# A third token block's output projection moved into the seven half-size products of the first two blocks, and those products moved later in the program

## The chip, the cores and the metric

The kernel runs on one core of one Trainium2 chip. Its time is in device microseconds. Engines are named as the profile names them: PE is TensorE (its matmuls), PEld its weight loads, DVE is VectorE, ACT ScalarE, POOL GpSimd, SP SyncE, which here only issues DMAs.

## What is computed

Two independent results are laid side by side. The first is attention with 32 query heads and one key and value head over 2048 tokens, followed by the output projection `@ wo`. The second is a two-dimensional Fourier transform by matrices, of which the real part is kept.

```python
q = (x @ wq).reshape(B, S, 32, 32).transpose(0, 2, 1, 3)
p = softmax(einsum("bhqd,bkd->bhqk", q, x @ wk) * 32 ** -0.5)
a = einsum("bhqk,bkd->bhqd", p, x @ wv).transpose(0, 2, 1, 3).reshape(B, S, 1024) @ wo
re, im = einsum("bsd,ed->bse", xb, hid_re), einsum("bsd,ed->bse", xb, hid_im)
b = einsum("ts,bse->bte", seq_re, re) - einsum("ts,bse->bte", seq_im, im)
return concatenate([a, b], axis=-1)
```

## The kernel before

Every large product is a sum of 128 x 128 by 128 x 512 matmuls in a reduced float format. To keep float32 accuracy, both operands are split into a high and a low part, and three matmuls are made of each pair: high by high, high by low, low by high. In the profile's names the right-hand parts are `rh` and `rl` (512 columns), the left-hand parts `mh` and `ml` (four 128 x 128 blocks in one tile), and the sum stands in a PSUM bank `psb`. I call one such matmul a fill. A group of fills fills one bank: eight row blocks by three give 24 fills, four row blocks by three give 12.

Attention runs in 32 units (4 token blocks `b` of 512 tokens, 8 groups `g` of 4 heads) of 32 steps. A step makes two score matmuls for the row maxima (`pss`, read by a reduction on DVE and an exponential on ACT), two score matmuls for the probabilities (`pst`, an exponential on ACT writes `p`), and, 3 times in a unit, a product of the probabilities with `v` (name `psb<-p,v`), which I call an attention product. DVE adds these into `ov`, and POOL multiplies by the inverse row sums `rb`. `level` (line 932) puts fills between the steps, so that a linear goal is met; the last 44 steps make no `pss` any more and take one fill more each.

The fills stand in one list `groups`, in this order: query projection, stage 1 and stage 2 of the Fourier part, and the output projection. Stage 1 and 2 use recursions that trade a product for additions. Stage 2 has seven products (`PRODUCTS`), each of 16 groups of 24 fills. The output projection of token blocks 0 and 1 uses the same kind of recursion (`OUTPUT`): the 8 token tiles are two halves of `MO` = 4 tiles, and seven half-size products of `MO` groups of 12 fills take the place of eight. Its left operands are sums of two tiles of the attention output, its right operands are sums of blocks of `wo`, split ahead by `w_parts`. `MID` is the place in stage 2's groups where these products are put in: behind 48 groups, so behind its third product. Token block 2 and then token block 3 use `o_group` instead: 8 groups of 24 fills for each block, with left operands that are stored already split (`oh`, `ol`), and right operands `wo_set`, 8 items of `wo` for each half of the columns.

Operands are made in two lines of work, `RL` for right-hand items and `ML` for left-hand ones. An item is loaded by a DMA of SP (`r`, `m`), two sources are added on POOL, POOL casts to the high part (`hi_r`, `hi_m`) and subtracts to get the low part (`lo`). The staging buffers `r` and `m` form rings of 3 (`NR0`, `NM0`, line 141), the split parts rings of `NR` = 14 right-hand and `NM` = 4 left-hand items (line 142). An item is due by its place among the fills (`due`), and `pump` takes the next steps when their time has come. Every engine's instructions are kept in the order in which the program writes them (line 79), SP's DMAs too, so an instruction that waits holds up all behind it on its engine.

Behind a finished group of stage 2's second half, DVE adds the bank to the first half's sum (`y<-y,psb`) and POOL adds or subtracts that into stored results (`y<-y,y`, twice for the last product). Behind all steps, the last 8 groups (block 3) run alone on PE: `first_part` takes 21 of the 24 fills, and the last 3 use the output of the last attention unit, which DVE splits.

Of the kernel before, what the change touches and what calls it, by code (L numbers as in the profile page):

```python
# [22 lines left out]
NG = 8  # L23
NQ = 4
NC = 16
MO = 4
MID = 3 * 16
ND = D // P


# [71 lines left out]
def tile_kernel(ctx: ExitStack, tc, xT, wq, wkv, wo, xbT, wT, cT, out):  # L102
# [12 lines left out]
    dram = ctx.enter_context(tc.tile_pool(name="dram", bufs=1, space=DRAM))  # L115
    qh_d = [[dram.tile([P, W], F32, name=f"qh_{b}_{g}") for g in range(NG)] for b in range(NQ)]
    ql_d = [[dram.tile([P, W], F32, name=f"ql_{b}_{g}") for g in range(NG)] for b in range(NQ)]
    o_d = [dram.tile([4, P, NG, P], F32, name=f"o_{b}") for b in range(2)]
    oh_d, ol_d = ({b: dram.tile([4, P, NG, P], F32, name=f"{n}_{b}") for b in (2, 3)} for n in ("oh", "ol"))
    w_d = [[[dram.tile([P, W], F32, name=f"w{q}_{n}_{c}") for q in range(2)] for c in range(4)] for n in range(len(OUTPUT))]  # L120
    c_d = {(i, e): [dram.tile([P, W], F32, name=f"c{i}{e}_{k}") for k in range(MO)] for i in range(2) for e in range(2)}
    r_d = [dram.tile([NC, P], F32, name=f"r_{u}") for u in range(NQ * NG)]
# [455 lines left out]
    def wo_set(e):  # L578
        return [Item([(lambda g=g: wo[g * P:(g + 1) * P, e * W:(e + 1) * W], 1)]) for g in range(NG)]
# [36 lines left out]

    got, made = [], []

    def o_products():

        seen = {}
        total = {(i, e): sum((i, e) == o[:2] for p in OUTPUT for o in p[2]) for i in range(2) for e in range(2)}
        for f, (lt, rt, outs) in enumerate(OUTPUT):
            def l_src(i, j, k):
                b, t = divmod(i * MO + k, 4)

                def src():
                    assert all(("o", b, g) in ready for g in range(4 * j, 4 * j + 4)), (b, t, j)
                    return o_d[b][t][:, 4 * j:4 * j + 4]
                return src  # L630

            R = [Item(None, pre=lambda f=f, c=c: have(("w", f, c), w_d[f][c])) for c in range(4)]
            for it in R:
                it.ahead = 24
            for k in range(MO):
                left = [Item([(l_src(i, j, k), sg) for i, j, sg in lt])]
                ys, plan = [], []
                for i, e, sg in outs:
                    n = seen.get((i, e, k), 0)
                    seen[i, e, k] = n + 1  # L640
                    it = None
                    if n:
                        it = Item([(lambda i=i, e=e, k=k, n=n: have(("c", i, e, k, n), c_d[i, e][k]), 1)])
                        ys.append(it)
                    r0 = (i * MO + k) * P
                    end_ = n + 1 == total[i, e]
                    plan.append((it, sg, out[r0:r0 + P, e * W:(e + 1) * W] if end_ else c_d[i, e][k], None if end_ else ("c", i, e, k, n + 1)))

                def post(ps, plan=plan):
                    first = None  # L650
                    for it, sg, to, key in plan:
                        if it is None:
                            if first is None:
                                first = op.tile([P, W], F32, name="qh")
                                dve.tensor_copy(first, ps)
                            store(to, first, key)
                            continue

                        def more(it=it, sg=sg, to=to, key=key):
                            (dve.tensor_add if sg > 0 else dve.tensor_sub)(it.y, it.y, ps)  # L660
                            store(to, it.y, key)
                        if it is plan[0][0]:
                            more()
                        else:
                            hold(more)
                yield Group(left, R, post, ys=ys, part=([R], 0))
# [3 lines left out]
    def o_group(b, t, e, ws):  # L670
        def post(ps):
            r0 = b * W + t * P
            to = out[r0:r0 + P, e * W:(e + 1) * W]
            if b < NQ - 1:
                oo = op.tile([P, W], F32, name="qh")
                dve.tensor_copy(oo, ps)
                store(to, oo)
                return

            n = len(halves)  # L680
            halves.append(n)
            oo = pp.tile([P, 2, W], F32, name="p")
            if n + 1 < 8:
                if n % 2:
                    dve.tensor_copy(oo[:, 0], ps)
                else:
                    act.activation(oo[:, 0], ps, AF.Copy)
                move(act, to, oo[:, 0])
                return
            for k, q in enumerate((act, sp)):  # L690
                cols = slice(k * W // 2, (k + 1) * W // 2)
                if k:
                    dve.tensor_copy(oo[:, k, :W // 2], ps[:, cols])
                else:
                    act.activation(oo[:, k, :W // 2], ps[:, cols], AF.Copy)
                move(q, to[:, cols], oo[:, k, :W // 2])
        return Group([o_left(b, t, q) for q in range(2)], ws, post)
# [10 lines left out]
    for it in st2[MID].right:  # L708
        it.back = 96
    rest += list(stage1()) + st2[:MID] + list(o_products()) + st2[MID:]  # L710
    w1, w0 = wo_set(1), wo_set(0)
    rest += [o_group(b, t, e, ws) for e, ws in ((1, w1), (0, w0)) for b in (2,) for t in range(4)]
    add(start + rest)
    w_parts(1010, 40)

# [103 lines left out]
    def pv(u, k):  # L819
# [11 lines left out]
        cur["at"] += 1  # L831
        if k == len(CUT) - 2:
            b, g = units[u]
            if b < 2:
                def scaled():
                    o = onp.tile([P, W], F32, name="oh")
                    gp.tensor_mul(o, ov[u], rb[u])
                    store(*blocks(o_d[b], g, o), ("o", b, g))
                ends.append(scaled)
                return  # L840
            hi_ = onp.tile([P, W], F32, name="oh").bitcast(F32R)
            lo_ = onp.tile([P, W], F32R, name="ol")
            lse["out"] = hi_, lo_

            last = u + 1 == len(units)
            e = dve if last else gp

            def low():
                e.tensor_sub(lo_, ov[u], hi_.bitcast(F32))
                if not last:  # L850
                    store(*blocks(oh_d[b], g, hi_))
                    store(*blocks(ol_d[b], g, lo_), ("o", b, g))

            ends.append(lambda: e.tensor_mul(ov[u], ov[u], rb[u]))
            ends.append(lambda: e.tensor_copy(hi_, ov[u]))
            ends.append(low)
# [82 lines left out]

    for n in range(total):  # L940
        u, r = divmod(n, SU)
        if n == total - 12:
            w1 = wo_set(1)
            add([o_group(NQ - 1, t, e, ws) for e, ws in ((0, w0), (1, w1)) for t in range(4)])
        score_step(n + SU + LEAD)
        if ends:
            ends.pop(0)()
        expo(n)
        if r == 16:
            inverse(u)  # L950
        if r in ENDS and n:
            pv((n - 1) // SU, (ENDS.index(r) - 1) % (len(CUT) - 1))
        level(n)
# [78 lines left out]
```

## Time and profile before

| | us |
|---|---|
| median of 3 runs | 2702.91 (2702.86 to 2704.59) |
| the profiled execution, its own time | 2701.05 |
| its span, first to last instruction | 2699.3 |
| PE busy in the span | 2691.8 |

The profiled execution is one execution. Its time is 1.75 us more than its span, and 1.86 us less than the median. A busy PE is read from matmul records whose ends are modelled, so the waits of PE and the spacing of matmuls are looked at beside it.

### The profile page before, as it was taken

The page shows a single profiled execution, that of the slowest core. Times are in us where ns is not written, and L with a number is a line of the kernel's source. Part 1 is how long each engine was busy: PE and PEld are TensorE (multiplying, and loading weights), DVE is VectorE, ACT ScalarE, POOL GpSimd, SP SyncE. Part 2 cuts the span into 40 slices and gives each one's busy share as a digit, 9 for nine tenths or more (in the row PEclk, how much of TensorE's full clock was granted, in tenths as well). Part 3 has the DMA queues.
Part 4 walks back from the last instruction along what each step waited for, and adds up shares of the span by engine and source line. Part 5 has one row for each costly group of instructions (what it writes and reads, how often), then busy time and mean ns, then how long its engine had stood idle before and what let it go on. Part 6 is the DMA issues. An engine that isn't in the chain of part 4 may idle for free.

```text
span 2699.3 us, 40577 instructions
## 1 busy us (share of the span) xinstructions
PE 2691.8 (100%) x13820; PEld 1918.1 (71%) x13820; DVE 1592.8 (59%) x1826; ACT 2134.8 (79%) x3131; POOL 1723.7 (64%) x1711
## 2 busy tenths in 40 slices
PE   9999999999999999999999999999999999999999
PEld 6876767676777767677776777667677776767767
DVE  5766666666666666565565656666565555655411
ACT  3588888888888888888888888888888888888741
POOL 4854425777547558765556675576887987865751
PEclk9999999999999999999999999999999999999999
DMA  8543336887788566564354588984675765644665
GB/s 277 190 136 128 114 97 202 282 285 233 241 268 281 203 226 195 175 193 142 125 160 152 183 258 278 306 262 128 213 226 161 223 199 159 209 142 134 192 211 187
DMA packets 316931, 538.24 MB, mean 199 GB/s; under 512 B 35962, under 2 KB 63354, under 8 KB 316666
## 3 DMA queue, kind: packets, MB, share of 16 engines
q1 hardware_dynamic: 315572, 533.69, 61.6%
q8 instruction: 109, 1.79, 0.3%
q10 hardware_dynamic: 1152, 1.97, 0.2%
q14 instruction: 98, 0.80, 0.1%
HBM read 395.58 MB, written 138.15 MB: 198 GB/s over the span
## 4 chain that ended last, share of the span: by engine, by line
PE 99%; ACT 0%; DVE 0%; DMA 0%; SPq 0%; issue 0%; ACTq 0%
PE psb L79 62%; PE pss L79 19%; PE pst L79 18%; ACT pss L79 0%; DVE nm L79 0%; DMA p<-in_xT_dram 0%; ACT p L79 0%; SPq L79 0%; DVE y L79 0%; DVE qh L79 0%; DVE rl L79 0%; ACT rh L79 0%; DVE p L79 0%; ACTq L79 0%
## 5 line engine op out<-in xcount | busy, mean ns | idle before, releaser
L79 DVE TENSOR_REDUCE nm<-pss 128x1 f32<-128x1024 f32 x1024 | 1252.5, 1223 | 562.0 <-PE pss L79 561.3
L79 ACT ACTIVATE p<-pst 128x1024 f32<-128x1024 f32 x1026 | 1056.6, 1030 | 437.7 <-PE pst L79 425.1
L79 ACT ACTIVATE pss<-pss,nm 128x1024 f32<-128x1024 f32 x1024 | 1114.7, 1089 | 57.2 <-DVE nm L79 55.5
L79 PE MATMUL psb<-rh,mh 128*128 128x512 f32 x1790 | 698.2, 390 | 0.3 <-ACT rh L79 0.3
L79 PE MATMUL psb<-rl,mh 128*128 128x512 f32 x1790 | 697.8, 390 | 0.6 <-DVE rl L79 0.5
L79 PE MATMUL psb<-rh,ml 128*128 128x512 f32 x1790 | 697.7, 390 | 0.0
L79 PE MATMUL pss<-kst,qst 128*128 128x512 f32 x2048 | 641.5, 394 | 0.2
L79 PE MATMUL pst<-qst,kst 128*128 128x512 f32 x2048 | 641.0, 394 | 0.5 <-ACT p L79 0.3
L79 POOL TENSOR_TENSOR ml<-m,mh 128x512 fp32r<-128x512 f32 x366 | 473.5, 1294 | 35.1 <-ACT mh L79 26.2
L79 PEld LDWEIGHTS pss<-kst,qst 128*128 128x128 f32 x2048 | 377.9, 188 | 125.4 <-issue 51.1
L79 PE MATMUL psb<-p,v 128*32 128x512 f32 x4096 | 459.3, 594 | 0.0
L79 PEld LDWEIGHTS pst<-qst,kst 128*128 128x128 f32 x2048 | 375.0, 188 | 103.0 <-ACT p L79 27.0
L79 PEld LDWEIGHTS psb<-rh,mh 128*128 128x128 f32 x1790 | 336.0, 188 | 75.6 <-ACT rh L79 1.8
L79 PEld LDWEIGHTS psb<-rl,mh 128*128 128x128 f32 x1790 | 336.0, 188 | 73.7 <-DVE rl L79 1.9
L79 PEld LDWEIGHTS psb<-rh,ml 128*128 128x128 f32 x1790 | 336.0, 188 | 71.1
L79 POOL CAST mh<-m 128x512 fp32r<-128x512 f32 x365 | 224.5, 615 | 229.1 <-PE psb L79 211.9
L79 PEld LDWEIGHTS psb<-p,v 128*32 128x32 f32 x4096 | 123.3, 110 | 283.0 <-issue 275.2
L79 POOL TENSOR_TENSOR m<-m,m 128x512 f32<-128x512 f32 x220 | 284.4, 1293 | 54.5 <-DMA m<-o 19.6
L79 POOL TENSOR_TENSOR rl<-r,rh 128x512 fp32r<-128x512 f32 x208 | 269.2, 1295 | 4.0
L79 POOL CAST rh<-r 128x512 fp32r<-128x512 f32 x208 | 129.0, 620 | 194.2 <-PE psb L79 147.3
L79 ACT ACTIVATION_READ_ACCUMULATOR pss<-pss,nm 128x1 f32 x1024 | 212.5, 207 | 0.0
L79 POOL TENSOR_TENSOR r<-r,r 128x512 f32<-128x512 f32 x120 | 155.1, 1293 | 52.3 <-DMA r<-in_wT_dram 33.6
(92 smaller groups left out, 791.3 us busy)
## 6 DMA issues: line engine op xcount, KB each, us to landing
m<-in_cT_dram SPq DMA_DIRECT2D x384, 256.0 KB
r<-s SPq DMA_DIRECT2D x192, 256.0 KB
y<-y SPq DMA_DIRECT2D x128, 256.0 KB
r<-in_wT_dram SPq DMA_DIRECT2D x88, 256.0 KB
m<-in_xbT_dram SPq DMA_DIRECT2D x88, 256.0 KB
y<-u SPq DMA_DIRECT2D x80, 256.0 KB
m<-in_wq_dram SPq DMA_DIRECT2D x64, 256.0 KB
qst<-qh SPq DMA_DIRECT2D x64, 256.0 KB
```

The source lines that it names most:

```text
L79: return lambda *a, **k: self.tc.keep_in_program_order(f(*a, **k))
```

## The change

Token block 2 joins the recursion. `MO` becomes 6: the 12 token tiles of blocks 0 to 2 are two halves of 6 (`token_tile` says which tile is which), and each of the seven products has 6 groups of 12 fills. Block 2's attention output is stored in float32 like that of blocks 0 and 1, so its split on POOL behind each unit goes, and its eight `o_group`s go. `MID` becomes 96: the seven products stand behind six products of stage 2, in front of the seventh. So stage 2's last product is the work that fills the last steps. Block 3 now makes both sets of `wo` items itself, and its groups are added 16 steps before the end of the steps, where it was 12.

```diff
--- before.py
+++ after.py
@@ -23,8 +23,8 @@
 NG = 8
 NQ = 4
 NC = 16
-MO = 4
-MID = 3 * 16
+MO = 6
+MID = 6 * 16
 ND = D // P
 
 
@@ -115,8 +115,8 @@
     dram = ctx.enter_context(tc.tile_pool(name="dram", bufs=1, space=DRAM))
     qh_d = [[dram.tile([P, W], F32, name=f"qh_{b}_{g}") for g in range(NG)] for b in range(NQ)]
     ql_d = [[dram.tile([P, W], F32, name=f"ql_{b}_{g}") for g in range(NG)] for b in range(NQ)]
-    o_d = [dram.tile([4, P, NG, P], F32, name=f"o_{b}") for b in range(2)]
-    oh_d, ol_d = ({b: dram.tile([4, P, NG, P], F32, name=f"{n}_{b}") for b in (2, 3)} for n in ("oh", "ol"))
+    o_d = [dram.tile([4, P, NG, P], F32, name=f"o_{b}") for b in range(3)]
+    oh_d, ol_d = ({b: dram.tile([4, P, NG, P], F32, name=f"{n}_{b}") for b in (3,)} for n in ("oh", "ol"))
     w_d = [[[dram.tile([P, W], F32, name=f"w{q}_{n}_{c}") for q in range(2)] for c in range(4)] for n in range(len(OUTPUT))]
     c_d = {(i, e): [dram.tile([P, W], F32, name=f"c{i}{e}_{k}") for k in range(MO)] for i in range(2) for e in range(2)}
     r_d = [dram.tile([NC, P], F32, name=f"r_{u}") for u in range(NQ * NG)]
@@ -616,13 +616,16 @@
 
     got, made = [], []
 
+    def token_tile(i, k):
+        return i * 4 + k if k < 4 else 4 + 2 * i + k
+
     def o_products():
 
         seen = {}
         total = {(i, e): sum((i, e) == o[:2] for p in OUTPUT for o in p[2]) for i in range(2) for e in range(2)}
         for f, (lt, rt, outs) in enumerate(OUTPUT):
             def l_src(i, j, k):
-                b, t = divmod(i * MO + k, 4)
+                b, t = divmod(token_tile(i, k), 4)
 
                 def src():
                     assert all(("o", b, g) in ready for g in range(4 * j, 4 * j + 4)), (b, t, j)
@@ -642,7 +645,7 @@
                     if n:
                         it = Item([(lambda i=i, e=e, k=k, n=n: have(("c", i, e, k, n), c_d[i, e][k]), 1)])
                         ys.append(it)
-                    r0 = (i * MO + k) * P
+                    r0 = token_tile(i, k) * P
                     end_ = n + 1 == total[i, e]
                     plan.append((it, sg, out[r0:r0 + P, e * W:(e + 1) * W] if end_ else c_d[i, e][k], None if end_ else ("c", i, e, k, n + 1)))
 
@@ -671,12 +674,6 @@
         def post(ps):
             r0 = b * W + t * P
             to = out[r0:r0 + P, e * W:(e + 1) * W]
-            if b < NQ - 1:
-                oo = op.tile([P, W], F32, name="qh")
-                dve.tensor_copy(oo, ps)
-                store(to, oo)
-                return
-
             n = len(halves)
             halves.append(n)
             oo = pp.tile([P, 2, W], F32, name="p")
@@ -708,8 +705,6 @@
     for it in st2[MID].right:
         it.back = 96
     rest += list(stage1()) + st2[:MID] + list(o_products()) + st2[MID:]
-    w1, w0 = wo_set(1), wo_set(0)
-    rest += [o_group(b, t, e, ws) for e, ws in ((1, w1), (0, w0)) for b in (2,) for t in range(4)]
     add(start + rest)
     w_parts(1010, 40)
 
@@ -831,7 +826,7 @@
         cur["at"] += 1
         if k == len(CUT) - 2:
             b, g = units[u]
-            if b < 2:
+            if b < NQ - 1:
                 def scaled():
                     o = onp.tile([P, W], F32, name="oh")
                     gp.tensor_mul(o, ov[u], rb[u])
@@ -939,8 +934,8 @@
 
     for n in range(total):
         u, r = divmod(n, SU)
-        if n == total - 12:
-            w1 = wo_set(1)
+        if n == total - 16:
+            w0, w1 = wo_set(0), wo_set(1)
             add([o_group(NQ - 1, t, e, ws) for e, ws in ((0, w0), (1, w1)) for t in range(4)])
         score_step(n + SU + LEAD)
         if ends:
```

Two stretches show how the instructions stand. The first is on POOL, in the last unit's steps, in the work that stands there beside the attention steps. Before, that is the end of stage 2's last product: one left-hand item's cast and subtraction, with the two additions into stored results between them.

```order
L79 CAST mh<-m_25431 128x512
L79 CAST rh<-r_25429 128x512
L79 TENSOR_TENSOR ml<-m_25431,mh 128x512
L79 TENSOR_TENSOR rl<-r_25429,rh 128x512
L79 CAST mh<-m_25470 128x512
L79 TENSOR_TENSOR y_25497<-y_25497,y_25495 128x512
L79 TENSOR_TENSOR y_25499<-y_25499,y_25495 128x512
L79 TENSOR_TENSOR ml<-m_25470,mh 128x512
```

Now, in the same product, the items of the `wo` set that was added at the 16th step from the end stand in the same gap (`r_25950`, `r_25952`, `r_25963` are their loads):

```order
L79 CAST mh<-m_25790 128x512
L79 TENSOR_TENSOR ml<-m_25790,mh 128x512
L79 CAST mh<-m_25820 128x512
L79 TENSOR_TENSOR y_25839<-y_25839,y_25837 128x512
L79 TENSOR_TENSOR y_25841<-y_25841,y_25837 128x512
L79 CAST rh<-r_25950 128x512
L79 CAST rh<-r_25952 128x512
L79 TENSOR_TENSOR rl<-r_25950,rh 128x512
L79 TENSOR_TENSOR rl<-r_25952,rh 128x512
L79 CAST rh<-r_25963 128x512
L79 TENSOR_TENSOR rl<-r_25963,rh 128x512
L79 TENSOR_TENSOR ml<-m_25820,mh 128x512
```

Three pairs of cast and subtraction moved in between the cast of a left-hand item (`m_25820`) and its subtraction.

The second stretch is SP's queue in the last block. Before, most loads of block 3's left-hand parts (`mh<-oh`, `ml<-ol`) stand without a load of `wo` (`r`) in front:

```order
L79 DMA r_26365<-in_wo_dram 128x512
L79 DMA mh<-oh_124 128x384
L79 DMA ml<-ol_126 128x384
L79 DMA mh<-oh_124 128x512
L79 DMA ml<-ol_126 128x512
L79 DMA r_26403<-in_wo_dram 128x512
L79 DMA mh<-oh_124 128x384
L79 DMA ml<-ol_126 128x384
L79 DMA mh<-oh_124 128x512
L79 DMA ml<-ol_126 128x512
L79 DMA r_26441<-in_wo_dram 128x512
```

Now a load of `wo` stands in front of each pair:

```order
L79 DMA r_26338<-in_wo_dram 128x512
L79 DMA mh<-oh_124 128x512
L79 DMA ml<-ol_125 128x512
L79 DMA r_26367<-in_wo_dram 128x512
L79 DMA mh<-oh_124 128x384
L79 DMA ml<-ol_125 128x384
L79 DMA r_26389<-in_wo_dram 128x512
L79 DMA mh<-oh_124 128x512
L79 DMA ml<-ol_125 128x512
L79 DMA r_26411<-in_wo_dram 128x512
L79 DMA mh<-oh_124 128x384
```

The loads moved here because the second set of `wo` is made in this stretch; block 2 used to share one of its two sets. On POOL, in the same stretch, there were only pairs of `wo` items:

```order
L79 CAST rh<-r_26241 128x512
L79 TENSOR_TENSOR rl<-r_26241,rh 128x512
L79 CAST rh<-r_26293 128x512
L79 TENSOR_TENSOR rl<-r_26293,rh 128x512
L79 CAST rh<-r_26365 128x512
L79 TENSOR_TENSOR rl<-r_26365,rh 128x512
```

Now the last additions of stage 2 into stored results stand between the cast and the subtraction of the first item of the second set (`r_26255`):

```order
L79 CAST rh<-r_26225 128x512
L79 TENSOR_TENSOR rl<-r_26225,rh 128x512
L79 CAST rh<-r_26255 128x512
L79 TENSOR_TENSOR y_26270<-y_26270,y_26268 128x512
L79 TENSOR_TENSOR y_26272<-y_26272,y_26268 128x512
L79 TENSOR_TENSOR rl<-r_26255,rh 128x512
L79 CAST rh<-r_26287 128x512
L79 TENSOR_TENSOR rl<-r_26287,rh 128x512
L79 CAST rh<-r_26338 128x512
L79 TENSOR_TENSOR rl<-r_26338,rh 128x512
```

The additions `y_26270` and `y_26272`, of stage 2's last group, moved in front of the subtraction that reads `r_26255`.

## Rows read from the trace of the kernel before

**Rows 1.** the page of the profile: span, busy time of the five engines, granted clock by slice
```profile
span 2699.3 us, 40577 instructions
...
PE 2691.8 (100%) x13820; PEld 1918.1 (71%) x13820; DVE 1592.8 (59%) x1826; ACT 2134.8 (79%) x3131; POOL 1723.7 (64%) x1711
...
PEclk9999999999999999999999999999999999999999
```

**Rows 2.** all waits of PE: first and last of five (total, times, longest us)
```profile
PE pst L79 <- DVE v L79: 1.5, 1, 1.5
...
PE psb L79 <- ACT rh L79: 0.3, 1, 0.3
```

**Rows 3.** timeline of PE, last block: 21 matmuls, first and last (start us, us)
```profile
2661.23 0.39 PE L79 MATMUL pst<-rh,mh 128*128 128x512 f32 x1
...
2665.76 0.39 PE L79 MATMUL pst<-rh,ml 128*128 128x512 f32 x1
```

**Rows 4.** stretch, length, busy us of PE, PEld, DVE, ACT, POOL; clock, DMA share, GB/s
```profile
1616.00:1788.00 172.00, 171.89 (x877) 121.74 (x876) 117.72 (x140) 144.18 (x215) 99.40 (x99) 1.00 0.89 295
...
2485.00:2577.00 92.00, 92.00 (x486) 63.07 (x485) 38.08 (x46) 64.15 (x88) 62.61 (x64) 1.00 0.61 192
...
2577.00:2650.00 73.00, 73.00 (x379) 48.94 (x378) 7.89 (x12) 30.34 (x30) 29.74 (x32) 1.00 0.64 210
```

**Rows 5.** timeline of POOL around 2560 us
```profile
2555.48 0.61 POOL L79 CAST mh<-m 128x512 fp32r<-128x512 f32 x1
...
2560.18 2.55 POOL L79 TENSOR_TENSOR y<-y,y 128x512 f32<-128x512 f32 x2 [4.09 <-DVE y L79]
...
2562.69 1.29 POOL L79 TENSOR_TENSOR ml<-m,mh 128x512 fp32r<-128x512 f32 x1
```

**Rows 6.** timeline of PE, same stretch
```profile
2555.02 0.39 PE L79 MATMUL psb<-rl,mh 128*128 128x512 f32 x1
...
2567.42 0.40 PE L79 MATMUL psb<-rh,ml 128*128 128x512 f32 x1
```

**Rows 7.** timeline of POOL: two right-hand items one behind the other
```profile
2608.51 0.61 POOL L79 CAST rh<-r 128x512 fp32r<-128x512 f32 x1 [12.45 <-PE psb L79]
...
2610.44 0.61 POOL L79 CAST rh<-r 128x512 fp32r<-128x512 f32 x1
```

**Rows 8.** timeline of PE: last attention product, first matmul of the last block
```profile
2644.42 4.50 PE L79 MATMUL psb<-p,v 128*32 128x512 f32 x40
...
2651.71 0.39 PE L79 MATMUL pss<-rh,mh 128*128 128x512 f32 x1
```

**Rows 9.** timeline of DVE behind that attention product
```profile
2648.98 0.69 DVE L79 TENSOR_TENSOR ov<-ov,psb 128x512 f32<-128x512 f32 x1 [6.49 <-PE psb L79]
...
2651.18 1.66 DVE L79 TENSOR_TENSOR ol<-ov,oh 128x512 fp32r<-128x512 f32 x1
...
2652.77 0.68 DVE L79 COPY qh<-psb 128x512 f32<-128x512 f32 x1
```

**Rows 10.** DVE subtractions of two SBUF operands, groups by shape (busy us, mean ns)
```profile
L79 DVE TENSOR_TENSOR rl<-p,rh 128x512 fp32r<-128x512 f32 x10 | 6.8, 690 | 0.6 <-ACT rh L79 0.4
...
L79 DVE TENSOR_TENSOR ol<-ov,oh 128x512 fp32r<-128x512 f32 x1 | 1.7, 1659 | 0.0
```

**Rows 11.** DMA issues of SP near the end
```profile
2631.78 0.38 SPq L79 DMA_DIRECT2D r<-in_wo_dram  x1
...
2651.67 0.32 SPq L79 DMA_DIRECT2D mh<-oh  x1
...
2652.09 0.38 SPq L79 DMA_DIRECT2D ml<-ol  x1
```

**Rows 12.** timeline of POOL: the operation that the first of those issues released
```profile
2635.08 0.61 POOL L79 CAST rh<-r 128x512 fp32r<-128x512 f32 x1 [7.92 <-DMA r<-in_wo_dram]
```

**Rows 13.** windows around the issues of 2651.67 us
```profile
2652.40:2654.30 1.90, 1.90 (x10) 1.59 (x9) 1.04 (x2) 0.00 (x0) 0.00 (x0) 1.00 0.59 207
...
2654.30:2655.20 0.90, 0.90 (x6) 0.74 (x5) 0.00 (x0) 0.00 (x0) 0.00 (x0) 1.00 0.00 0
```

## Prediction

> **What bounds the kernel now.** I read the page first: PE is busy for 2691.8 of 2699.3 us at a granted clock of 9 or more tenths in all 40 slices [rows 1]. A busy PE could still be a slow one, so I looked next at the waits of PE: five groups, 3.3 us in all, the longest 1.5 us and the smallest 0.3 us [rows 2]; those named there fall into the first few microseconds and the joints. So PE works without a gap, in the order of the program. Then the timeline of PE: in the last block 21 matmuls start 4.53 us apart from first to last, so one fill takes 4.53 / 20 = 0.2267 us [rows 3]. PE is the bound, and a fill less is worth 0.2267 us, as long as nothing that PE waits for comes later than it does now. The windows show that the others have room on average: where the seven products stood, POOL was busy for 99.4 of 172 us and DVE for 117.7, and PE for 171.89 [rows 4].
>
> **What is saved.** The first three blocks took 7 x 4 x 12 = 336 fills in the seven products and 8 x 24 = 192 in block 2's own groups, 528. Now they take 7 x 6 x 12 = 504. That is 24 fills less, 24 x 0.2267 = **5.44 us**. The steps' other matmuls stay, and the fills that are gone are spread over all steps.
>
> The Trainium skill (TensorE: Matmul & The Clock Gate, section Back-to-back issue gap) gives about 131 ns per matmul of 512 columns for a sustained stream of weight loads and matmuls. By it 24 fills would be worth an estimated 3.1 us. The trace has 226.7 ns for just such a stream, and I go by it.
>
> **What is added beside PE.** The seven products have 14 groups more, so 14 left-hand items more on POOL. A cast and a subtraction take 1.93 us, from one cast to the next [rows 7]. That is 27 us, and five of the seven products also add two sources, 10 additions of 1.25 us (two start 2.51 us before what follows them [rows 5]), 12 us. Against it, block 2's split goes (8 units, 1.93 each) and one of three `wo` sets (8 items), 31 us. POOL gains some 9 us over the kernel. DVE gets 24 additions more and 8 copies less, 16 x 0.69 [rows 9] = 11 us. Both are hidden: the products ran at 58% of POOL with 0.1 us of idle PE [rows 4]. What hides them is the distance in the rings, so a price appears only where several POOL operations stand in a row in front of one that PE waits for. I looked for that place by place in the order of POOL: in the kernel before, at most 5.1 us of other work (worked out with 1.25 us for an addition or a subtraction and the other 0.68 of the 1.93 for a cast) stands between the cast of a left-hand item and its subtraction. In the changed one a single place goes far above this, the first of the two shown in the part on the change.
>
> **The first new wait.** Before, in the same product and at the same pace (no `pss` any more), the cast starts at 2555.48 us, when the ring frees its tile: PE's last use of the old content starts at 2555.02. Then POOL waits for DVE's addition, runs two additions from 2560.18, and the subtraction from 2562.69 to 2563.98. PE reads the result at 2567.42 [rows 5, 6]. So 3.44 us are left, with no attention product between release and use to lengthen them. The changed program has the same pattern: 54 matmuls from the last use of the ring's tile to the one that reads `ml`, 54 x 0.2267 = 12.24 us, against 12.40 before. But three items of the `wo` set, due at once when their groups are added, stand between the two additions and the subtraction: 3 x 1.93 = 5.79 us [rows 7]. PE comes to wait 5.79 - 3.44 = **2.35 us**. Behind it the later items follow: the next one is needed 12 fills and a `pst` pair later, and one pair of `wo` stands between items, so POOL catches up and I see no second wait there. The bounds: nothing, if the loads for the pairs came so early that POOL could run them before DVE's addition (the order on POOL excludes it: they stand behind the additions); and some 1 us more, if they come late, since these loads queue behind others (a load issued at 2631.78 released POOL at 2635.08, 3.3 us later [rows 11, 12]). I take 2.35.
>
> **The last block.** Let P be the start of the last attention product, 2644.42; the last block starts at P + 7.29 [rows 8]. DVE's addition into `ov` starts at P + 4.56, its split's subtraction at P + 6.76, and the next instruction on DVE at P + 8.35 [rows 9]. That one is now the last addition of stage 2, and POOL waits for it with two additions in front of the subtraction of the first item of the new set. With that the queue of SP is held up too: the fourth load of the set (`r_26367`) waits for this subtraction (ring of 3 buffers), and behind it stand the left-hand parts for the second half of the second group. POOL's two additions take 2.5 us and the subtraction 1.25.
>
> How late DVE is depends on its subtraction: 1659 ns there, against 690 ns for ten others of this form [rows 10]. In the run before, POOL worked at that moment; now it would stand idle, waiting. I take 0.69: DVE's addition then ends near P + 8.2, POOL's subtraction near P + 12.0, and SP issues the pair at about P + 12.4 and 12.85. A pair issued at 2651.67 and 2652.09 has moved its bytes by 2654.3, when traffic stops: 2.2 us behind the second issue [rows 11, 13]; behind a load of 256 KB at most the 3.3 us of the row above. So the second part lands between P + 15.0 and P + 16.2. PE wants it 35 fills into the block, at P + 7.29 + 35 x 0.2267 = P + 15.2. The first wait is 0 to 1.0 us. The six halves behind it have a load of `wo` in front as well, and at 9 or 12 fills each (2.0 or 2.7 us) they need 640 or 768 KB in that time, so some waits of 0 to 0.3 us may follow. I take **0.8 us** in all, between 0 and 3.
>
> The Trainium skill (SBUF — State Buffer, section Who interferes with whom) says that a DVE instruction with two SBUF inputs and a GpSimd instruction that reads SBUF share one port, and that the second to come is blocked. The two durations of this subtraction agree with it; no run here yet has it with POOL idle. Were it 1.66 us again, the wait in the last block would be about 1 us longer.
>
> **The sum.** -5.44 + 2.35 + 0.8 = -2.3 us. The profiled execution's span of 2699.3 would become 2697.0 and its own time of 2701.05 would be 2698.8; on the median of 2702.91, which lies 1.86 us above that execution, the same step gives **2700.6 us**, a ratio of 0.9991. A change of this kernel under about 0.2% (5.4 us, from 2697.5 to 2708.3) can hardly be told from none, so I call this no change.
>
> **Rivals.**
> - *The full gain* (1 in 10): nothing waits, 2702.91 - 5.44 = 2697.5 us, just at the border. For it speaks that PE hardly waits anywhere now. Against it speaks 5.79 us of work in a gap of 3.44. It needs the burst to start earlier than the additions, and the order is fixed.
> - *SP's queue holds up the last block* (1 in 7): each half's parts wait for a `wo` buffer, and loads land as slowly as 3.3 us and more behind each other. The first pair then lands near P + 16.2 or later and each half behind it adds 0.3 to 0.5 us, in all 3 to 5 us. With the 2.35 the time is 2702.8 to 2704.8. From 3.1 us of waits in the last block on, the change is a loss; for a loss of over 0.2% these would have to come to 8.5 us, over 1 us for each of the seven halves, and the 3.3 us row doesn't give that. Against it speaks that the kernel before loads four pairs in that block without a wait, but only two loads of `wo` with them.
> - *Saved fills are worth nothing* (1 in 20): another engine would set the pace of a step, and the time would be 2702.9 plus the new waits, so up to 2706. Against it: PE has 0.1 us of idle time in three stretches of 337 us together [rows 4].
> - *A wait that I didn't see*, where the products now stand or behind it (1 in 10): every group there has its two or three POOL operations as before, and the block of `wo` products takes no POOL for its right-hand items. I give it 1 to 6 us.
>
> The forecast has 6 in 10, with 2699.8 to 2702.3 as its own range (a first wait of 2.35 to 3.35, and 0 to 1.5 in the last block). For 8 in 10 I leave out the ends beyond the full gain and the upper half of the losses: 2697.3 to 2704.0. Faster by over 0.2% takes the better half of the full gain and a little for the scatter of the median, 0.10; slower by over 0.2% the far end of the last three rivals, 0.05; the rest is no change.
>
> **What would show it.** The waits of PE would have a new line, POOL's `ml`, of 2 to 3 us, some 83 us before the end, and behind it the timeline of POOL with six operations on `rh` and `rl` in a row. In the last block PE would wait for `mh` or `ml` by DMA for less than 1 us at a time. DVE's subtraction `ol` would take 0.69 us. The number of fills would be 24 less at the same spacing. The prediction is wrong if PE shows no wait on POOL (then the gap was longer than in the rows), if the last block waits over 3 us, or if waits show around the moved products.

## The result, and the profile after

The changed kernel takes **2706.93 us** (median of 22 runs, 2704.39 to 2709.19) against 2702.7 us for the kernel before (median of 22 runs). The ratio is 1.0015, with a 95% interval of 1.0008 to 1.0021: about 4 us slower, where 2700.6 was predicted and 2704.0 was the upper end. The profiled execution has a span of 2705.2 us and its own time of 2706.98, close to the median. The profiled execution of the kernel before ran 1.65 us below its median of 2702.7, so the two profiles lie 5.9 us apart and the medians 4.2.

The page of the changed kernel, answering to [rows 1]:

```profile
span 2705.2 us, 40586 instructions
...
PE 2693.0 (100%) x13796; PEld 1912.7 (71%) x13796; DVE 1599.1 (59%) x1840; ACT 2131.7 (79%) x3131; POOL 1730.7 (64%) x1717
...
PEclk9999999999999999999999999999999999999999
```

The saving is there: 13820 - 13796 = 24 matmuls less. Yet PE is busy 1.2 us longer, and out of work for 2705.2 - 2693.0 = 12.2 us, where it was 7.5. So some matmuls are late, and with fewer of them and more busy time some look slow too. Tenths over 40 slices of 67 us are too coarse to show either. The waits of PE tell where (total, times, longest), against the five of 3.3 us in [rows 2]:

```profile
PE psb L79 <- POOL ml L79: 3.0, 1, 3.0
...
PE pss L79 <- ACT pss L79: 0.9, 1, 0.9
PE pst L79 <- DMA mh<-oh: 0.8, 1, 0.8
...
PE pss L79 <- DMA mh<-oh: 0.5, 1, 0.5
```

Four new lines, at three places. The first, and the last two, are the places that the prediction named. The `ACT pss` line is not.

**Place one, 2614 us: the items of `wo`.** The timeline of POOL (start, us, and in brackets the idle time before and what ended it):

```profile
2606.69 2.54 POOL L79 TENSOR_TENSOR y<-y,y 128x512 f32<-128x512 f32 x2 [4.20 <-DVE y L79]
2609.37 0.61 POOL L79 CAST rh<-r 128x512 fp32r<-128x512 f32 x1
2611.07 0.61 POOL L79 CAST rh<-r 128x512 fp32r<-128x512 f32 x1 [1.09 <-DMA r<-in_wo_dram]
...
2614.14 0.61 POOL L79 CAST rh<-r 128x512 fp32r<-128x512 f32 x1
...
2616.04 1.26 POOL L79 TENSOR_TENSOR ml<-m,mh 128x512 fp32r<-128x512 f32 x1
```

Between the two additions and `ml` stand the three pairs of `wo` operations that the prediction counted (two of the subtractions in one row of 2.54 us, not shown, and one of 1.26), with 1.09 us of waiting for a load in their midst. It is the late load that was the upper bound. PE in the same stretch:

```profile
2613.99 0.39 PE L79 MATMUL psb<-rl,mh 128*128 128x512 f32 x1
2617.36 0.50 PE L79 MATMUL psb<-rh,ml 128*128 128x512 f32 x1 [2.98 <-POOL ml L79]
...
2619.51 0.63 PE L79 MATMUL psb<-rl,mh 128*128 128x512 f32 x1
...
2621.64 0.56 PE L79 MATMUL psb<-rh,mh 128*128 128x512 f32 x1
2622.04 0.39 PE L79 MATMUL psb<-rl,mh 128*128 128x512 f32 x1
```

The reader is to see two things. The fill at 2617.36 starts 3.37 us behind the one before it, where 0.2267 is usual [rows 3]: 3.14 us late. And 2.2 us later the fills stand 0.426 us apart (2619.51 to 2621.64, five steps in 2.13 us), not 0.2267, until 2622.04. The windows have the granted clock as the column behind POOL:

```profile
2400.00:2450.00 50.00, 48.96 (x254) 32.70 (x253) 31.66 (x34) 39.13 (x59) 31.97 (x32) 1.00 0.87 296
...
2618.50:2622.00 3.50, 3.50 (x10) 2.72 (x9) 0.00 (x0) 1.03 (x1) 3.50 (x4) 0.51 0.86 265
2650.00:2670.00 20.00, 18.69 (x93) 13.06 (x86) 3.19 (x5) 0.00 (x0) 15.16 (x17) 1.00 0.79 241
```

0.51 in that stretch is the lower of the clock's two levels, 1.2 GHz. A busy share of 3.50 of 3.50 hides it. Six fills at 0.2 us each and a slow `pst` pair (0.85 us at 2618.66, where 0.45 is usual) make it cost about 1.6 us.

The Trainium skill (TensorE: Matmul & The Clock Gate, section Back-to-back issue gap) has matmuls of 512 columns 512 / 1.2 = 427 ns apart at the lower level. The spacing in this trace, 0.426 us, agrees. The same page (Part 1: The HAM clock gate) says that the engine falls to this level when it has been idle. Here it fell behind a wait of 2.98 us; not every such wait was followed by a fall (last section).

**Place two, 2437 us: the wait that was not foreseen.** It lies in the last of the seven products. The profile names ACT. Followed back, it goes through three other engines. PE's timeline first:

```profile
2436.77 0.39 PE L79 MATMUL psb<-rh,mh 128*128 128x512 f32 x1
2438.02 0.73 PE L79 MATMUL pss<-kst,qst 128*128 128x512 f32 x2 [0.86 <-ACT pss L79]
2438.94 0.74 PE L79 MATMUL pst<-qst,kst 128*128 128x512 f32 x2 [0.19 <-ACT p L79]
```

The timeline of ACT has the exponential that PE waits for:

```profile
2436.76 1.09 ACT L79 ACTIVATE pss<-pss,nm 128x1024 f32<-128x1024 f32 x1 [1.35 <-DVE nm L79]
```

And that of DVE has what ACT waits for:

```profile
2434.24 1.28 DVE L79 TENSOR_TENSOR y<-y,psb 128x512 f32<-128x512 f32 x2 [1.22 <-PE pst L79]
2435.45 2.35 DVE L79 TENSOR_REDUCE nm<-pss 128x1 f32<-128x1024 f32 x2
```

ACT waits for a reduction (`nm`), which stands on DVE behind two additions `y<-y,psb`, which started late. The name in their bracket is of no use, since they read no `pst`: they read a bank of fills and `y`, and the chain that ended last puts their start down to the load of `y`, issued at 2428.47:

```profile
2428.47 5.58 DMA y<-c
```

Why the load was so late, SP's issues say first:

```profile
2410.47 0.91 SPq L79 DMA_DIRECT2D r<-s  x2
2420.19 0.32 SPq L79 DMA_DIRECT2D m<-o  x1
...
2428.47 0.98 SPq L79 DMA_DIRECT2D y<-c  x2
```

and then the timeline of POOL:

```profile
2417.63 1.29 POOL L79 TENSOR_TENSOR ov<-ov,rb 128x512 f32<-128x512 f32 x1 [8.16 <-DVE ov L79]
2418.87 1.29 POOL L79 TENSOR_TENSOR ml<-m,mh 128x512 fp32r<-128x512 f32 x1
```

POOL stands for 8.16 us before the multiplication by the inverse row sums, which waits for the last attention product of a unit. The subtraction `ml` behind it doesn't need that product, but has to wait in order. Until it has read its buffer, SP can't issue the next `m<-o` (from 2411.4 to 2420.19 it issues nothing), and all of SP's later issues are pushed together. In the end PE, which was busy for 50.00 of the 50 us from 2400 to 2450 in the kernel before, is busy for 48.96. It loses 1.02 us at 2438.02 (1.25 from start to start, where 0.23 is usual) and 0.6 at the next two pairs.

Such a stop was to be seen in the kernel before, in the timeline of POOL at the old place of the products, without a price:

```profile
1634.47 1.29 POOL L79 TENSOR_TENSOR ov<-ov,rb 128x512 f32<-128x512 f32 x1 [6.91 <-DVE ov L79]
```

The changed kernel itself has a longer stop, 80 us earlier among the same moved products:

```profile
2337.35 1.29 POOL L79 TENSOR_TENSOR ov<-ov,rb 128x512 f32<-128x512 f32 x1 [8.93 <-DVE ov L79]
```

SP issues nothing from 2329.17 to 2339.91 there, and yet PE is busy for all of 2320 to 2360. So a stop of POOL has no price by itself. Two differences are to be seen in SP's issues. Around 2417 the loads for stage 2's last product (`r<-s`, six from 2410 to 2431) stand among the others, and some groups need two loads of `y`; around 2337 there is no `r<-s`, and `y` is loaded one at a time. No run separates the two.

**Place three, the last block.** The timeline of DVE, which answers to [rows 9]:

```profile
2654.43 0.69 DVE L79 TENSOR_TENSOR ol<-ov,oh 128x512 fp32r<-128x512 f32 x1
2655.49 0.69 DVE L79 TENSOR_TENSOR y<-y,psb 128x512 f32<-128x512 f32 x1 [0.38 <-PE psb L79]
```

POOL waits for that addition, and its subtraction for POOL's own two:

```profile
2656.26 2.54 POOL L79 TENSOR_TENSOR y<-y,y 128x512 f32<-128x512 f32 x2 [3.19 <-DVE y L79]
2658.76 1.28 POOL L79 TENSOR_TENSOR rl<-r,rh 128x512 fp32r<-128x512 f32 x1
```

SP's issues behind that subtraction:

```profile
2660.07 0.33 SPq L79 DMA_DIRECT2D r<-in_wo_dram  x1
...
2660.97 0.38 SPq L79 DMA_DIRECT2D ml<-ol  x1
```

And PE, which waits for the second half's parts and for those of the next:

```profile
2663.41 0.50 PE L79 MATMUL pss<-rh,mh 128*128 128x512 f32 x1 [0.53 <-DMA mh<-oh]
...
2666.56 0.47 PE L79 MATMUL pst<-rh,mh 128*128 128x512 f32 x1 [0.78 <-DMA mh<-oh]
```

The chain is the predicted one, step by step. The windows have PE out of work for 1.31 us in 2650 to 2670.

**The account.** I took each distance from one start of a PE instruction to the next, less the usual one of its form, and summed by stretch: 3.1 us at the first wait, 1.85 behind it (all fills slower than usual up to 2623), 2.6 in 2400 to 2450, 2.5 in the last block, 1.3 in pieces too small for the list of waits. Less 5.44 that is +5.9 us, as the spans have it (2705.2 - 2699.3). This is one execution of each kernel.

### The profile page after: what moved, and what is told of

The parts are those of the page before. It is cut to its first block, busy times and chain, and to the rows that moved or that the text cites. A ratio compares the mean times of both kernels' runs of the same rounds, so it can differ in the third digit from the quotient of the medians.

```text
span 2705.2 us, 40586 instructions
## 1 busy us (share of the span) xinstructions
PE 2693.0 (100%) x13796; PEld 1912.7 (71%) x13796; DVE 1599.1 (59%) x1840; ACT 2131.7 (79%) x3131; POOL 1730.7 (64%) x1717
## 4 chain that ended last, share of the span: by engine, by line
PE 97%; DMA 1%; POOL 0%; DVE 0%; ACT 0%; issue 0%; SPq 0%; POOLq 0%; DVEq 0%; ACTq 0%
PE psb L79 61%; PE pss L79 19%; PE pst L79 18%; SPq L79 0%; DVE nm L79 0%; DMA out_dram<-y 0%; DMA y<-c 0%; DMA p<-in_xT_dram 0%; ACT pss L79 0%; DMA r<-in_wo_dram 0%; DMA mh<-oh 0%; POOL ml L79 0%; ACT p L79 0%; POOL rl L79 0%; POOL y L79 0%
## 5 line engine op out<-in xcount | busy, mean ns | idle before, releaser
L79 POOL TENSOR_TENSOR ml<-m,mh 128x512 fp32r<-128x512 f32 x380 | 490.6, 1291 | 43.9 <-ACT mh L79 26.6
L79 POOL CAST mh<-m 128x512 fp32r<-128x512 f32 x379 | 232.5, 614 | 273.3 <-PE psb L79 248.6
L79 POOL TENSOR_TENSOR m<-m,m 128x512 f32<-128x512 f32 x230 | 296.9, 1291 | 29.1 <-DMA m<-in_xbT_dram 9.2
L79 POOL TENSOR_TENSOR rl<-r,rh 128x512 fp32r<-128x512 f32 x200 | 258.3, 1292 | 3.5
L79 POOL CAST rh<-r 128x512 fp32r<-128x512 f32 x200 | 122.9, 615 | 137.4 <-PE psb L79 121.6
```

The source lines that it names most:

```text
L79: return lambda *a, **k: self.tc.keep_in_program_order(f(*a, **k))
```

## The experiments

Ten kernels ran. Ratios are to the kernel before, with 95% intervals; differences in us are between medians, for which the changed kernel's own interval of 2.2 to 5.7 us above before says how far to trust them.

**Adding block 3's groups 40 steps ahead of the end, not 16.** The due times of the `wo` items then spread over more fills, so no three are due at once.

```diff
-        if n == total - 16:
+        if n == total - 40:
```

> The changed kernel, with the last block's groups added 40 steps before the end of the steps in place of 16, so that the wo items are made one by one when they are due. Theory: the wait of 2.98 us on POOL goes, and with it the 3.5 us behind it at a granted clock of 0.51, which cost some 1.9 us; the time falls by about 5.0 us, to 2702 us. Rival 1: the low clock has another cause and stays, or comes elsewhere; then only 3.1 us go, to 2703.8. Rival 2: PE arrives earlier at the last block and waits there for what the first wait had covered; then the time stays near 2706.9.

Measured: 2703.09 us, 1.0003 [0.9994, 1.0012], 3.8 us faster than the changed kernel. The wait on POOL's `ml` is gone, PE is busy for 10.00 of 10.00 us in 2610 to 2620, and the clock is 1.00 there:

```profile
2610.00:2620.00 10.00, 10.00 (x44) 7.64 (x43) 0.69 (x1) 5.43 (x6) 10.00 (x11) 1.00 0.65 185
```

So the wait came from the `wo` items that stood together, and the slow fills behind it went with it. The gain of 3.8 lies between the theory's 5.0 and the 3.1 of rival 1, and the profile has what that rival says: the low clock came elsewhere. The wait at 2437 us was longer in this profile, and now that one had the slow clock behind it. PE's timeline:

```profile
2439.34 0.73 PE L79 MATMUL pss<-kst,qst 128*128 128x512 f32 x2 [1.96 <-ACT pss L79]
```

and the window behind it:

```profile
2439.60:2443.20 3.60, 3.42 (x9) 2.40 (x9) 2.05 (x3) 3.38 (x5) 3.60 (x4) 0.56 0.99 376
```

**Spreading the last product's first right-hand items over 192 fills, not 96.** `back` sets how far ahead of their group these items may be due.

```diff
-        it.back = 96
+        it.back = 192
```

> The changed kernel, with the right-hand items of stage 2's last product spread over 192 fills in place of 96. Theory: the waits near 2437 us (some 2.6 us with what follows) come from the two loads and the additional POOL addition of each of these items, crowded into the last two of the seven products on SP's queue and on POOL; spread, they go, and the time is about 2704.3 us. Rival: SP's queue is held up there by POOL's wait of 8.2 us for an attention product alone, whatever the density; then the wait stays and the time is 2706.9.

Measured: 2717.26 us, 1.0051 [1.0038, 1.0064], 10 us slower still (the median of 5 runs, where the other kernels have 11). Neither the theory nor the rival has this. The wait in the seven products grew to 5.3 us, with the clock at 0.58 behind it (2444 to 2448 us), and POOL's `ml` wait stayed (2.6 us). That more lead helps is refuted. SP issues nothing from 2411.35 to 2420.83 and from 2424.91 to 2431.75, each time in front of an `m<-o`; in the changed kernel that happens once there. That the `r<-s` loads, spread further ahead, make it worse is a reading of this and not shown.

**Loading the last block's left-hand parts from ACT's queue.** This takes them out from behind SP's loads of `wo`.

```diff
-    pos = {"fill": 0, "s": 0}
+    pos = {"fill": 0, "s": 0, "late": False}
...
+        q = sp
         if len(h.shape) == 3:
...
-        move(sp, it.hi, h)
-        move(sp, it.lo, l)
+            q = act if pos["late"] else sp
+        move(q, it.hi, h)
+        move(q, it.lo, l)
...
     take(last[0].at - pos["fill"] - 12)
+    pos["late"] = True
```

> The changed kernel, with the left-hand parts of the last block loaded from ACT's queue in place of SP's. Theory: the pairs of loads wait in SP's queue behind loads of wo that wait for POOL; from another queue they are in time, the waits of 0.5 and 0.8 us in the last block go, with the slower matmuls around them, and the time falls by 1.5 to 2.5 us to about 2705. Rival: the bytes of this stretch are the limit; the waits stay within 0.3 us and the time too.

Measured: 2706.03 us, 1.0012 [1.0004, 1.0021]. The time alone, 0.9 us less where 1.5 to 2.5 was expected, doesn't tell it from the changed kernel. The profile does: PE is busy for all of 2650 to 2670 and no DMA is in the list of its waits. So SP's order was the cause in the last block. The profile also has POOL's wait of 2.6 us without a slow clock behind it, and one at 2441 us (2.0, `ACT pss`) with one. The windows:

```profile
2442.40:2445.60 3.20, 3.20 (x9) 2.48 (x8) 2.07 (x4) 2.28 (x5) 3.20 (x5) 0.52 1.01 367
...
2621.20:2625.00 3.80, 3.77 (x16) 2.92 (x16) 0.00 (x0) 1.03 (x1) 3.80 (x5) 1.00 0.67 208
2650.00:2670.00 20.00, 20.00 (x109) 13.99 (x109) 3.19 (x5) 0.00 (x0) 15.01 (x16) 1.00 0.86 280
```

**The move alone:** the kernel before, its seven products with four groups each and block 2's own groups kept, but in the late place.

```diff
-MID = 3 * 16
+MID = 6 * 16
```

> The kernel before, with the seven products of blocks 0 and 1 moved in front of stage 2's last product and nothing else changed. Theory: the move alone brings the waits around the products (2.6 us), and neither the wait on POOL in the last steps nor the waits in the last block; 2705.3 us, against 2702.7 of the kernel before. Rival: those waits come from the 14 groups more and not from the place; then 2702.7 us, within 0.5.

Measured: 2708.53 us, 1.0023 [1.0014, 1.0032], 5.9 us slower than before, with no fill saved. That is more than theory and rival gave. So the place by itself costs, by the medians, more than the whole change does. Its longest wait, 4.1 us, is of the unforeseen kind, again behind DVE's addition into a late `y`, whose load SP issued at 2358.50. DVE's timeline:

```profile
2363.84 0.69 DVE L79 TENSOR_TENSOR y<-y,psb 128x512 f32<-128x512 f32 x1 [4.63 <-issue]
2364.44 2.35 DVE L79 TENSOR_REDUCE nm<-pss 128x1 f32<-128x1024 f32 x2
```

and PE's:

```profile
2367.01 1.14 PE L79 MATMUL pss<-kst,qst 128*128 128x512 f32 x2 [4.11 <-ACT pss L79]
```

Two things stand in front of that load here, and no run tells them apart. POOL's stop is only 3.07 us. SP issues nothing until 2345.66, in front of an `m<-o`, and then four loads `r<-s` for stage 2's last product take SP from 2348.05 to 2353.71, the last of them waiting for POOL's work on earlier items. Its second wait, 1.2 us at 817 us, lies long before either place of the products.

**POOL's multiplication written later.** The work behind a unit's last attention product is taken up from step 6 of the next unit on, by when the product is done, and what stands behind on POOL can go ahead.

```diff
-        if ends:
+        if ends and r >= 6:
             ends.pop(0)()
```

> The changed kernel, with POOL's scaling and split of an attention unit's output put five steps later (at the steps 6 to 8 of the next unit in place of 1 to 3), so that POOL doesn't stand waiting for the attention product with a left-hand item's subtraction behind it. Theory: that wait (8.2 us of POOL) holds up the load of the next left-hand tile on SP, that load the y load behind it, that one DVE and ACT, and so PE near 2437 us; with the scaling later SP isn't held, DVE's y load comes in time, and the wait of 0.9 to 2.1 us with the slow matmuls behind it goes: 2.6 to 4 us less, 2703 to 2704.3 us, with the wait on POOL's ml in the last steps unchanged. Rival: the r loads and additions of stage 2's last product alone are too many for SP and POOL there; then the wait stays, and the time is 2706.9.

Measured: 2705.82 us, 1.0012 [1.0003, 1.0021]. By time, 1.1 us less where 2.6 to 4 was expected, this is not told from the changed kernel. In the profile the wait is gone: POOL's multiplication comes without a wait, SP issues `m<-o` at 2412.94 (it was 2420.19), and PE is busy for 49.96 of the 50 us (it was 48.96) and 4.96 of the five around the old wait. POOL's timeline:

```profile
2423.35 1.29 POOL L79 TENSOR_TENSOR ov<-ov,rb 128x512 f32<-128x512 f32 x1
```

and the windows:

```profile
2400.00:2450.00 50.00, 49.96 (x260) 33.78 (x259) 32.44 (x35) 40.41 (x60) 33.26 (x34) 1.00 0.92 309
2435.00:2440.00 5.00, 4.96 (x22) 3.72 (x21) 3.95 (x5) 4.92 (x8) 3.17 (x3) 1.00 1.08 391
```

So the chain through POOL and SP is shown in the profile as the cause of place two: without the stop, with the `r<-s` loads as many as before, the wait doesn't come. The stop at 2337 that cost nothing says that it takes more than the stop. Part of the gain went back at place one, where POOL's wait is 3.3 us here.

**The same edit in the kernel before,** as a control.

> The kernel before, with POOL's scaling put five steps later and nothing else changed: a control for the run with that edit. It had no wait of PE that this edit could take away, so 2702.6 us within 0.5 by every theory; a gain here would say that the edit helps by something else.

Measured: 2702.12 us, 0.9997 [0.9988, 1.0006]: no change that the interval tells. By the medians it is 0.9 us less, about as much as the same edit gave in the changed kernel, so the times don't show what the edit is worth in the late place. The profile does, by the wait that is gone.

**The seven products behind stage 2,** not in front of its last product, and no `back`.

```diff
-MID = 6 * 16
+MID = 7 * 16
...
-    for it in st2[MID].right:
-        it.back = 96
```

> The changed kernel, with the seven products behind all of stage 2 in place of in front of its last product. Theory: the r loads and POOL additions of stage 2's last product no longer meet the two loads and results per group of the seven products, and in the last steps stand products that give POOL no additions into stored results, so neither the wait near 2437 us nor the wait on POOL's ml near the end comes: the saved fills show, 2697.5 to 2699 us, with some 1.5 us left in the last block. Rival: the place in the program isn't the cause, and the products bring their wait with them to the last steps, where there is less other work between fills; then 2704 us or more.

Measured: 2703.33 us, 1.0002 [0.9993, 1.0011], 3.6 us faster than the changed kernel, between the theory (2699 at most) and the rival (2704 at least). Neither the wait at 2437 nor POOL's `ml` is left. Instead DVE waits for late `y` loads at the very end (one of 3.12 us at 2619.42) and PE for DVE twice, 3.6 us in all, and once for POOL's `rl`, 1.2. With the products moved once more, the late loads of `y` move with them. The waits of PE:

```profile
PE psb L79 <- DVE y L79: 3.6, 2, 2.3
...
PE psb L79 <- POOL rl L79: 1.2, 1, 1.2
```

**The three cures together:** 40 steps, step 6, ACT's queue.

> The changed kernel with three edits at once: the last block's groups added 40 steps before the end, POOL's scaling five steps later, the last block's left-hand parts loaded from ACT's queue. Theory: these three waits and the low clock behind them are all that eats the 24 saved fills; without them the time is the 2702.6 of the kernel before less 5.4, 2697.2 us, within 1. Rival: a fill less isn't worth 0.2267 us, or further waits come up behind these; then 2700 us or more.

Measured: **2699.62 us, 0.9987 [0.9978, 0.9996]**, faster than the kernel before by 3.4 us and than the changed kernel by 7.3. That is 2.4 us above the theory and just under the rival's 2700. Of the new waits one of 0.3 us is left, and the clock is 1.00 in all three places, so the waits were the cause of the loss, but not all of the 5.44 came out. The waits of PE:

```profile
PE pss L79 <- DMA ml<-ol: 0.3, 1, 0.3
```

and the windows:

```profile
2400.00:2450.00 50.00, 49.99 (x259) 33.83 (x259) 32.44 (x35) 40.44 (x59) 33.31 (x34) 1.00 0.92 301
2610.00:2620.00 10.00, 10.00 (x57) 6.35 (x59) 0.69 (x1) 4.82 (x5) 10.00 (x11) 1.00 0.77 220
2650.00:2670.00 20.00, 20.00 (x90) 16.52 (x89) 0.69 (x1) 0.22 (x1) 16.76 (x17) 1.00 0.82 262
```

**What 24 fills are worth.** The kernel before without the last of block 2's eight groups: one tile of the output is not computed.

```diff
-    rest += [o_group(b, t, e, ws) for e, ws in ((1, w1), (0, w0)) for b in (2,) for t in range(4)]
+    rest += [o_group(b, t, e, ws) for e, ws in ((1, w1), (0, w0)) for b in (2,) for t in range(4 if e else 3)]
```

> The kernel before without the last of token block 2's eight groups: 24 fills less, and one 128 x 512 tile of the output isn't computed. It measures by itself what 24 fills are worth. By my first term, 24 x 0.2267 = 5.4 us: 2697.2 us. Rival: part of the time of a fill is taken up again by the other work of the steps, and 3 to 4 us come out, as in the run with the three edits (2699 us).

Measured: 2698.44 us, 0.9985 [0.9977, 0.9994]: 4.2 us less by the medians, and 1.6 to 6.2 by the interval. Its profile has one wait of 1.0 us for a store, at 1783 us, which the kernel before lacks. So 5.44 stands within, and "worth nothing" is excluded; the lower price of 3.1 us that the prediction put beside it is not excluded by this run, only by the spacing in the trace.

**The three cures without `back`:** is the lead of 96 fills still needed?

```diff
-        it.back = 96
+        it.back = 0
```

> The kernel with the three edits, and the right-hand items of stage 2's last product spread over the last of the seven products alone (72 fills in place of 96), which has one source per left-hand item. Theory: two-source left-hand items and these items together crowd SP and POOL; apart from each other the 1 us of small waits near 2420 us goes, and the time is 2698.6 us. Rival: closer together they come too late, and a wait of 1 to 3 us comes up behind the products: 2701 to 2703 us.

Measured: 2707.41 us, 1.0017 [1.0008, 1.0026], 7.8 us slower than with it. PE waits 2.0 us at 2464.76, 2.1 at 2495.39 (both for ACT) and 1.4 for DVE's `y`, and the clock averages 0.79 and 0.81 in the 8 and 7 us around the first two. So the lead is needed, and of 0, 96 and 192 fills (the last tried without the cures) the 96 is best.

## Why the prediction was wrong

- **What bounds the kernel: right.** PE, fill by fill. The losses in the account are delays of PE.
- **24 fills for 5.44 us: borne out in size.** The fills are gone, and taking 24 away by themselves gave 4.2 us, taking them away with the cures 3.4. Both intervals hold 5.44 (the second reaches 5.9). The prediction's quotient 4.53 / 20 is 0.2265, not 0.2267; 24 fills are 5.44 by either. Why the medians are below it is open. In the first the wait for a store takes 1.0 of it; in the second no new wait over 0.3 us is left, so what is missing lies in pieces too small for the list of waits. Against the kernel before with the step-6 edit (2702.12), which has one of the three cures, the gain is only 2.5.
- **The first new wait, 2.35 us: right in place and mechanism.** It was 2.98, because the load came late by 1.09, the case that I put at "some 1 us more" and didn't take (the gap was some 0.3 us wider than 3.44). What I left out is what such a wait costs behind it: 1.6 us of slow fills. The prediction priced a wait at its own length, and looked at the clock only to see that it was at 9 or more tenths.
- **The last block, 0.8 us (0 to 3): right in mechanism, too small.** 1.3 us by the waits, 2.5 by the distances. Two halves waited, and the matmuls behind each wait began slowly. DVE's subtraction took 0.69 us with POOL idle, as assumed.

The Trainium skill (SBUF — State Buffer, section Who interferes with whom) has a VectorE instruction with two SBUF inputs compete for a shared read interface with a GpSimd instruction that reads SBUF. The 0.69 us beside a waiting POOL agrees.

- **The step that failed:** "Both are hidden", and with it the rival "A wait that I didn't see", at 1 in 10, with the reason that every group there "has its two or three POOL operations as before". The busy times held (POOL 7.0 us more where 9 were expected, DVE 6.3 where 11 were); the averages are not what failed. I went through the order of POOL and counted the operations in front of each subtraction. But what stands in front can also be an operation that itself waits. POOL's stops at the multiplication (6.91 us and more in the old place) were in the trace, and I had not asked what queues behind them on POOL, then on SP, then for `y` on DVE. The move alone, which saves no fill, cost 5.9 us. The experiment at step 6 shows the chain in the changed kernel; in the move alone that edit was not tried, and its late `y` load stands behind a shorter stop and four `r<-s` loads. I had priced the move by operations at 0.1 us of idle PE in the old place [rows 4], and the same pattern doesn't cost the same elsewhere. Waits around the moved products are what the prediction itself named as a sign of being wrong. With 2.6 us here and 1.85 for the slow fills, the sum turns from -2.3 to about +2; the rest is the sizes above and the small pieces.
- **Luck:** the change stayed under the border of 0.2% below which the prediction called it no change. That is not to the credit of its working, which had 3.15 us of losses against the 5.44, where the account has 11.35. And the border was drawn too wide: a loss of 4.2 us could be told from none.
- **Left open:** why the same stop had no price in the old place, nor at 2337 us in the changed kernel. The loads `r<-s` of stage 2's last product and the groups with two loads of `y`, both found at 2417 and not at 2337, are my guess, not shown. Also open is why the wait at 2437 us was 0.9 us in one profile and 2.0 in two others with the same code there.

## What to carry to other kernels

Follow an engine's order not only by how much work stands in front of an operation, but by what each operation in front waits for: an in-order engine that stops for 8 us at something unrelated also stops the DMA queue that waits for its buffers, and the price, where there is one, appears some engines further on, under another's name. When a block of work is moved, run the move alone first; here it cost more than the saving was worth, and three small changes of order (one load queue, one step, one due time) turned +4.2 us into -3.4. And price a wait of a busy PE with what may come behind it at the lower clock, not by its length alone.

## What was not expected of the hardware

Behind some waits of PE of a few microseconds the granted clock was at its lower level for about 3 us (0.50 to 0.58 in windows of this length), and fills took 0.426 us in place of 0.227, some 1.6 us in all. It followed the waits of 2.98 us and 1.96 us shown above, one of 2.0 at 2441 us in the kernel with ACT's queue, one of 3.3 (0.50 in 2616.80 to 2619.70 in the step-6 kernel), the 4.1 us of the move alone (0.52 in 2367.00 to 2370.40), the 5.3 us with 192 fills of lead, the 2.0 and 2.1 us without lead (0.50 in 2466.90 to 2469.80 and in 2497.40 to 2500.30), and the 2.3 us of the products behind stage 2 (0.64 in 2623.00 to 2626.00). It did not follow the wait of 2.59 us in the kernel with ACT's queue (1.00), nor one of the same length with 192 fills of lead (1.00 in 2626.60 to 2632.00), nor the 0.86 us in the changed one (1.00). So the length of the wait alone doesn't decide it in these runs, and they don't show what does.
